# Attention and MLP on one core: attention steps as one skewed stream, groups of varied size, loads reordered, k of the first tiles on a second DMA queue

## The chip, the cores and the metric

One Trainium2 chip, one of its cores. The metric is the device time of one execution in microseconds (us). Executions of one kernel mostly agree within 1%; times below are medians of all runs of a kernel. A run that is more than 1.5% above the fastest of its kernel is called slow and is left out of the ratios. The span of a profiled execution is 1.7 to 2.1 us shorter than its time, so medians are compared with medians and spans with spans. Engines: PE (matmul), DVE (vector), ACT (scalar), POOL (GpSimd), SP (issues DMAs).

## The reference, cut to what matters

Block-wise linear attention with decay per head, then layer norm, a two-layer MLP with relu and a residual.

```python
# q, k, v: (4, 8, 768, 64) f32; lam: (8,)
# attention, in blocks, per batch and head:
#   out = ((q k^T) * decay_mask) v  +  (q * lam^(i+1)) S
#   S   = lam^block * S + (k * lam^(block-1-j))^T v
# x = out, heads side by side: (4, 768, 512)
xn = (x - mean) / sqrt(var + 1e-6) * g_ln
out = x + relu(xn @ w_ch1) @ w_ch2        # 512 -> 2048 -> 512, float32 out
```

Of the kernel before, what the change touches and what calls it, by code (L numbers as in the profile page):

```python
# [7 lines left out]
F32 = mybir.dt.float32  # L8
BF16 = mybir.dt.bfloat16
I32 = mybir.dt.int32  # L10
ALU = mybir.AluOpType
ACT = mybir.ActivationFunctionType
# [4 lines left out]
def kernel(  # L17
# [11 lines left out]
    nc = tc.nc  # L29
    B, H, S, D = q.shape  # L30
    C = 128
    nb = S // C
    NT = B * nb
    DM = H * D
    DF = moe_w_ch1.shape[1]
    NP = H // 2
    KA = DM // 128
    KB = DF // 128
    GT = 4
    NG = NT // GT  # L40
    NWC = 4
# [3 lines left out]
    ctx.enter_context(tc.manual_schedule())  # L45

    const = ctx.enter_context(tc.tile_pool(name="const", bufs=1))
    wst = ctx.enter_context(tc.tile_pool(name="wst", bufs=4))
    inp = ctx.enter_context(tc.tile_pool(name="inp", bufs=6))
    wk = ctx.enter_context(tc.tile_pool(name="wk", bufs=3))  # L50
    xp = ctx.enter_context(tc.tile_pool(name="xp", bufs=12))
    gp = ctx.enter_context(tc.tile_pool(name="gp", bufs=2))
    ps = ctx.enter_context(tc.tile_pool(name="ps", bufs=1, space=PSUM))

# [3 lines left out]
    def load_tile(t):  # L58
        b, c = divmod(t, nb)
        got = []  # L60
        for name, src in (("q", q), ("k", k), ("v", v)):
            f = inp.tile([128, H, D], F32, tag=name + "in", name=name + "in")
            nc.sync.dma_start(f, src[b, :, c * C:(c + 1) * C, :].rearrange("h p d -> p h d"))
            got.append(f)
        qkv_in[t] = got

    w1 = const.tile([128, KA, DF], BF16)
    w2 = const.tile([128, KB, DM], BF16)
    w_stage = {}
    W1C = DF // NWC  # L70
    W2K = KB // NWC

    def load_w1(c):
        f = wst.tile([128, KA, W1C], F32, tag="wst", name="w1f")
        nc.sync.dma_start(f, moe_w_ch1[:, c * W1C:(c + 1) * W1C].rearrange("(k p) f -> p k f", p=128))
        w_stage["w1", c] = f

    def load_w2(c):
        f = wst.tile([128, W2K, DM], F32, tag="wst", name="w2f")
        nc.sync.dma_start(f, moe_w_ch2[c * W2K * 128:(c + 1) * W2K * 128, :].rearrange("(k p) d -> p k d", p=128))  # L80
        w_stage["w2", c] = f

    def cast_w1(c):
        f = w_stage.pop(("w1", c))
        for kk in range(KA):
            dst = w1[:, kk, c * W1C:(c + 1) * W1C]
            if kk % 2 == 0:
                nc.vector.tensor_scalar_mul(dst, f[:, kk, :], g_col[:, kk:kk + 1])
            else:
                nc.scalar.mul(dst, f[:, kk, :], g_col[:, kk:kk + 1])  # L90

    def cast_w2(c):
        f = w_stage.pop(("w2", c))
        hk = W2K // 2
        nc.vector.tensor_copy(w2[:, c * W2K:c * W2K + hk, :], f[:, 0:hk, :])  # L95
        nc.gpsimd.tensor_copy(w2[:, c * W2K + hk:(c + 1) * W2K, :], f[:, hk:, :])

    lam_b = const.tile([128, H], F32)
    nc.sync.dma_start(lam_b, lam[None, :].to_broadcast([128, H]))
    load_tile(0)  # L100
    g_col = const.tile([128, KA], F32)
    nc.sync.dma_start(g_col, moe_g_ln.rearrange("(k p) -> p k", p=128))
    load_tile(1)
    load_w1(0)
    load_tile(2)
    load_tile(3)
    load_w1(1)
    load_w1(2)
    load_w1(3)


    ident = const.tile([128, 128], BF16)
    nc.gpsimd.memset(ident, 0.0)
    nc.gpsimd.affine_select(
        out=ident, in_=ident, compare_op=ALU.not_equal, fill=1.0,
# [5 lines left out]
        out=tril, in_=tril, compare_op=ALU.is_ge, fill=0.0,  # L121
# [35 lines left out]
    xT_of = {}  # L157

    def bf_inputs(t):
        qf, kf, vf = qkv_in.pop(t)  # L160
        qb = wk.tile([128, H, D], BF16, tag="qb", name="qb")
        nc.gpsimd.tensor_copy(qb, qf)  # L162
        kb = wk.tile([128, H, D], BF16, tag="kb", name="kb")
        nc.gpsimd.tensor_copy(kb, kf)  # L164
        vb = wk.tile([128, H, D], BF16, tag="vb", name="vb")
        nc.gpsimd.tensor_tensor(vb, vf, lam_v[:, :, None].to_broadcast([128, H, D]), op=ALU.mult)  # L166
        st[t] = dict(qb=qb, kb=kb, vb=vb)

    def p1(t):
        s = st[t]  # L170
        tp = ps.tile([128, 2, NP, 128], BF16, tag="aux", bufs=2, name="tp")
        for i, src in enumerate((s["kb"], s["qb"])):
            for p in range(NP):
                nc.tensor.transpose(tp[:, i, p, :], src[:, 2 * p:2 * p + 2, :], ident)  # L174
        kT = kTp[t % 2]
        nc.scalar.copy(kT[0:64, :, 0, :], tp[0:64, 0, :, :])  # L176
        qT = wk.tile([128, NP, 128], BF16, tag="qT", name="qT")
        nc.vector.tensor_copy(qT, tp[:, 1, :, :])  # L178
        nc.scalar.copy(kT[64:128, :, 1, :], tp[64:128, 0, :, :])  # L179
        s["kT"], s["qT"] = kT, qT  # L180

    def p2(t):
# [53 lines left out]

    def p4(t):
        s = st.pop(t)
        g, i = divmod(t, GT)
        if i == 0:  # L240
            xT_of[g] = gp.tile([128, KA, GT * 128], BF16, tag="xT", name="xT")
        xt = ps.tile([128, KA, 128], BF16, tag="aux", bufs=2, name="xt")
        for kk in range(KA):
            nc.tensor.transpose(xt[:, kk, :], s["xc"][:, kk * 128:(kk + 1) * 128], ident)  # L244
        nc.scalar.copy(xT_of[g][:, :, i * 128:(i + 1) * 128], xt)  # L245


    def mlp_units(g):
        hT = gp.tile([128, KB, GT * 128], BF16, tag="hT", name="hT")

        def m1(n):
            p1_ = ps.tile([128, GT * 128], F32, tag="mm", bufs=3, name="pm1")
            for kk in range(KA):
                nc.tensor.matmul(p1_, lhsT=w1[:, kk, n * 128:(n + 1) * 128], rhs=xT_of[g][:, kk, :],  # L254
                                 start=(kk == 0), stop=(kk == KA - 1))
            nc.scalar.activation(hT[:, n, :], p1_, ACT.Relu)  # L256

        acc = {}

        def m2(i, part):  # L260
            t = g * GT + i
            if part == 0:
                acc[i] = ps.tile([128, DM], F32, tag="mm", bufs=3, name="pm2")
            for kk in range(part * 4, part * 4 + 4):
                nc.tensor.matmul(acc[i], lhsT=hT[:, kk, i * 128:(i + 1) * 128], rhs=w2[:, kk, :],  # L265
                                 start=(kk == 0), stop=(kk == KB - 1))
            if part == KB // 4 - 1:
                x, rstd = x_keep.pop(t)
                o = wk.tile([128, DM], F32, tag="o", name="o")
                nc.vector.scalar_tensor_tensor(o, in0=acc.pop(i), scalar=rstd, in1=x, op0=ALU.mult, op1=ALU.add)  # L270
                b, c = divmod(t, nb)
                nc.sync.dma_start(out[b, c * C:(c + 1) * C, :], o)

        for n in range(KB):
            yield lambda n=n: m1(n)
        for i in range(GT):
            for part in range(KB // 4):
                yield lambda i=i, part=part: m2(i, part)


    def p01(t):
        if t + 1 < NT:
            bf_inputs(t + 1)
        p1(t)

    def att_steps(tiles):
        n = len(tiles)
        seq = []
        for j in range(n + 1):
            if j < n:  # L290
                seq.append((p01, tiles[j]))
            if j > 0:
                seq.append((p4, tiles[j - 1]))
            if j < n:
                seq.append((p2, tiles[j]))
                seq.append((p3, tiles[j]))
        return seq

    next_load = [4]

    def load_next():
        if next_load[0] < NT:
            load_tile(next_load[0])
            next_load[0] += 1


    load_next()
    bf_inputs(0)
    for f, t in att_steps(list(range(GT))):
        f(t)  # L310
    cast_w1(0)
    load_w2(0)
    load_next()
    load_w2(1)
    load_next()
    load_w2(2)
    load_next()
    load_w2(3)
    load_next()

    for g in range(NG):
        tiles = list(range((g + 1) * GT, min((g + 2) * GT, NT)))
        steps = att_steps(tiles)
        units = list(mlp_units(g))
        for u, unit in enumerate(units):
            if g == 0:
                if u % 4 == 0 and u // 4 + 1 < NWC:
                    cast_w1(u // 4 + 1)
                if u in (6, 9, 12, 15):
                    cast_w2(u // 3 - 2)  # L330
            if u % 8 == 0:
                load_next()
            unit()
            if u % 2 == 1 and u // 2 < len(steps):
                f, t = steps[u // 2]
                f(t)
        for f, t in steps[len(units) // 2:]:
            f(t)


# [28 lines left out]
```

## The kernel before: the parts that the change touches

The kernel works on 24 tiles of 128 rows (6 per sequence). `bf_inputs` casts a tile's q, k, v to bf16 on POOL (qb, kb, vb); `p1` transposes k and q on PE and copies them out (kT, qT); `p2` makes the masked scores mA and the state S; `p3` makes the output x and its norm (xc); `p4` transposes the normed x (xT). In the MLP pm is a matmul's PSUM tile and hT the hidden layer. Groups of four tiles then go through the MLP, with the attention of the next group interleaved between units of four matmuls of 512 columns.

```python
def bf_inputs(t):
    qf, kf, vf = qkv_in.pop(t)
    nc.gpsimd.tensor_copy(qb, qf)                                   # POOL
    nc.gpsimd.tensor_copy(kb, kf)                                   # POOL
    nc.gpsimd.tensor_tensor(vb, vf, lam_v[...], op=ALU.mult)        # POOL
# ...
def p2(t):
    # scores on PE, two mA on DVE, state product pk on PE ...
    if c == 0:                                                      # first tile of a sequence
        nc.vector.tensor_tensor(Sn, pk, lamC, op=ALU.mult)
    else:
        nc.vector.tensor_tensor(tmp, pk, state["S"], op=ALU.add)    # Stmp, DVE
        nc.gpsimd.tensor_tensor(Sn, tmp, lamC, op=ALU.mult)         # Sn, POOL
# (the last tile of a sequence has no Sn)
# ...
def p01(t):
    if t + 1 < NT:
        bf_inputs(t + 1)      # the casts of the NEXT tile come first
    p1(t)

# per tile, in program order: p01(t), p4(t-1), p2(t), p3(t)
for g in range(NG):           # six groups of four
    for u, unit in enumerate(units):
        # ... casts of weights in the first group, next load ...
        unit()
        if u % 2 == 1 and u // 2 < len(steps):
            f, t = steps[u // 2]
            f(t)
```

## Time and profile before

| | before |
|---|---|
| median of 4 runs | 259.62 us (258.76 to 262.1) |
| span of the profiled execution | 258.8 us |
| busy: PE, DVE, ACT, POOL | 86%, 53%, 42%, 31% |
| first MLP matmul | 34.4 us |
| first MLP group | 45.8 us |
| four groups of four tiles | 36.7 to 36.9 us each |
| last group, and the last store | 27.8 and 3.8 us |

The prediction shows how these are read out of the chain of waits. Columns of the timeline: start, duration (us), engine, line, operation, output and input, shape, count, and in brackets the idle time before it and what ended it.

### The profile page before, as it was taken

How to read it: one execution, taken by the hardware profiler on the slowest of the kernel's cores; microseconds unless marked ns; L12 is line 12 of the kernel's file. 1: busy time of each engine (PE TensorE's matmuls, PEld its weight loads, DVE VectorE, ACT ScalarE, POOL GpSimd, SP SyncE). 2: the span in 40 equal slices, each digit the busy share in tenths (PEclk: the TensorE clock that was granted, in tenths of full speed). 3: DMA queues.
4: the chain of work that ended last, by engine and by line, in shares of the span. 5: the costliest groups of instructions: out<-in, count | busy, mean ns of one | idle time of the engine just before them, and what ended most of it. 6: DMA issues, size and time to landing. Idle time of an engine off the chain costs nothing.

```text
span 258.8 us, 4115 instructions
## 1 busy us (share of the span) xinstructions
PE 223.7 (86%) x1600; PEld 122.3 (47%) x1600; DVE 137.8 (53%) x256; ACT 108.9 (42%) x207; POOL 81.0 (31%) x101
## 2 busy tenths in 40 slices
PE   0666479695997999989999979999979999989994
PEld 0444235352553555545555535555535555444441
DVE  3467766762753746773475664548547467600121
ACT  5332266743114664306662326761146742066200
POOL 3546052754413523740051352810145131000000
PEclk9999759998899999999999999999999999999999
DMA  6999929999999920279901549601210002110022
GB/s 128 273 227 360 270 64 292 254 276 287 218 241 252 222 56 0 84 162 203 203 2 43 127 120 228 136 0 43 81 42 3 0 3 81 41 43 0 0 81 81
DMA packets 83250, 33.81 MB, mean 131 GB/s; under 512 B 76064, under 2 KB 76064, under 8 KB 83232
## 3 DMA queue, kind: packets, MB, share of 16 engines
q1 hardware_dynamic: 83232, 33.57, 55.8%
q8 instruction: 12, 0.20, 0.3%
q14 instruction: 6, 0.05, 0.1%
HBM read 27.27 MB, written 6.29 MB: 130 GB/s over the span
## 4 chain that ended last, share of the span: by engine, by line
PE 66%; DVE 16%; ACT 9%; DMA 4%; issue 2%; POOL 1%; SPq 1%; POOLq 0%
PE pm L265 28%; PE pm L254 23%; PE sc L190 4%; DVE stats L225 4%; DVE x L222 4%; PE tp L174 3%; DMA w2f<-in_moe_w_ch_dram 3%; ACT hT L256 2%; DVE mA L192 2%; ACT kTp L179 2%; PE po L215 2%; PE po L219 2%; PE xt L244 2%; DVE xc L229 2%; DMA kin<-in_k_dram 2%
## 5 line engine op out<-in xcount | busy, mean ns | idle before, releaser
L254 PE MATMUL pm<-xT,w 128*128 128x512 bf16 x384 | 92.3, 384 | 6.9 <-ACT xT L245 4.0
L265 PE MATMUL pm<-w,hT 128*128 128x512 bf16 x384 | 90.9, 382 | 3.0 <-DVE w L95 2.7
L256 ACT ACTIVATE hT<-pm 128x512 bf16<-128x512 f32 x96 | 54.4, 597 | 19.7 <-PE pm L254 19.5
L254 PEld LDWEIGHTS <-w 128*128 128x128 bf16 x384 | 36.3, 99 | 45.5 <-issue 9.2
L265 PEld LDWEIGHTS <-hT 128*128 128x128 bf16 x384 | 36.0, 98 | 39.6 <-issue 3.7
L207 POOL TENSOR_TENSOR Sn<-Stmp,lamC 128x512 bf16<-128x512 f32 x16 | 20.6, 1289 | 98.9 <-DVE Stmp L206 50.4
L270 DVE SCALAR_TENSOR_TENSOR o<-pm,rstd,x 128x512 f32<-128x512 f32 x24 | 17.8, 741 | 48.2 <-PE pm L265 48.2
L231 ACT ACTIVATE std<-mv,eps_t 128x1 f32<-128x1 f32 x24 | 7.1, 294 | 85.2 <-DVE mv L227 85.2
L192 DVE TENSOR_TENSOR mA<-sc,tril 128x512 bf16<-128x512 f32 x48 | 30.8, 683 | 22.3 <-PE sc L190 22.3
L166 POOL TENSOR_TENSOR vb<-vin,lam_v 128x512 bf16<-128x512 f32 x24 | 25.9, 1079 | 6.9 <-issue 4.4
L178 DVE COPY qT<-tp 128x512 bf16<-128x512 bf16 x24 | 10.1, 422 | 24.1 <-ACT kTp L176 24.1
L222 DVE TENSOR_TENSOR x<-po,lam_q 128x512 f32<-128x512 f32 x24 | 16.6, 690 | 11.6 <-PE po L219 9.8
L162 POOL CAST qb<-qin 128x512 bf16<-128x512 f32 x24 | 15.2, 632 | 19.6 <-DMA qin<-in_q_dram 19.6
L190 PE MATMUL sc<-qT,kTp 128*128 128x128 bf16 x192 | 17.8, 234 | 3.2 <-DVE qT L178 1.7
L179 ACT COPY kTp<-tp 64x512 bf16<-64x512 bf16 x24 | 13.9, 580 | 15.5 <-DVE qT L178 15.5
L229 DVE TENSOR_SCALAR xc<-x,mv 128x512 bf16<-128x512 f32 x24 | 18.4, 767 | 0.9
L244 PE MATMUL xt<-ident,xc 128*128 128x128 bf16 x96 | 10.0, 231 | 10.2 <-DVE xc L229 10.2
L190 PEld LDWEIGHTS <-kTp 128*128 128x128 bf16 x192 | 13.7, 104 | 10.8 <-ACT kTp L179 5.3
L225 DVE BATCH_NORM_STATS2 stats<-x 128x6 f32<-128x512 f32 x24 | 16.7, 694 | 0.8
L245 ACT COPY xT<-xt 128x512 bf16<-128x512 bf16 x24 | 14.1, 587 | 6.1 <-PE xt L244 5.9
L174 PE MATMUL tp<-ident,kb 128*128 128x128 bf16 x96 | 10.5, 238 | 6.9 <-POOL kb L164 6.9
L164 POOL CAST kb<-kin 128x512 bf16<-128x512 f32 x24 | 15.2, 632 | 3.5 <-DMA kin<-in_k_dram 2.9
(42 smaller groups left out, 146.9 us busy)
## 6 DMA issues: line engine op xcount, KB each, us to landing
qin<-in_q_dram SPq DMA_DIRECT2D x24, 256.0 KB, 5.0
kin<-in_k_dram SPq DMA_DIRECT2D x24, 256.0 KB, 5.3
vin<-in_v_dram SPq DMA_DIRECT2D x24, 256.0 KB, 5.1
out_dram<-o SPq DMA_DIRECT2D x24, 256.0 KB, 2.0
w1f<-in_moe_w_ch_dram SPq DMA_DIRECT2D x4, 1024.0 KB, 7.5
w2f<-in_moe_w_ch_dram SPq DMA_DIRECT2D x4, 1024.0 KB, 6.8
lam_b<-in_lam_dram SPq DMA_DIRECT2D x1, 4.0 KB, 2.8
g_col<-in_moe_g_ln_dram SPq DMA_DIRECT2D x1, 2.0 KB, 4.1
```

What stands on the lines that cost most here:

```text
L166: nc.gpsimd.tensor_tensor(vb, vf, lam_v[:, :, None].to_broadcast([128, H, D]), op=ALU.mult)
L174: nc.tensor.transpose(tp[:, i, p, :], src[:, 2 * p:2 * p + 2, :], ident)
L179: nc.scalar.copy(kT[64:128, :, 1, :], tp[64:128, 0, :, :])
L190: nc.tensor.matmul(sc[:, i, :], lhsT=s["kT"][:, h // 2, h % 2, :], rhs=s["qT"][:, h // 2, :], start=(i == 0), stop=(i == H // 2 - 1), skip ...
L192: nc.vector.tensor_tensor(mA[:, half * (H // 2):(half + 1) * (H // 2), :], sc, tril[:, None, :].to_broadcast([128, H // 2, 128]), op=ALU.mult)
L207: nc.gpsimd.tensor_tensor(Sn, tmp, lamC, op=ALU.mult)
L222: nc.vector.tensor_tensor(x.rearrange("p (h d) -> p h d", h=H), po, lam_q[:, :, None].to_broadcast([128, H, D]), op=ALU.mult)
L225: nc.vector.bn_stats(stats, x)
L229: nc.vector.tensor_scalar(xc, x, mv[:, 0:1], None, op0=ALU.subtract)
L254: nc.tensor.matmul(p1_, lhsT=w1[:, kk, n * 128:(n + 1) * 128], rhs=xT_of[g][:, kk, :], start=(kk == 0), stop=(kk == KA - 1))
L256: nc.scalar.activation(hT[:, n, :], p1_, ACT.Relu)
L265: nc.tensor.matmul(acc[i], lhsT=hT[:, kk, i * 128:(i + 1) * 128], rhs=w2[:, kk, :], start=(kk == 0), stop=(kk == KB - 1))
```

## The change

Intent: PE should not wait at the end of a group. The attention steps become one list for all tiles, skewed by one tile (p3 of tile t-1 after p1 of tile t, so that PE need not wait for mA), and spread evenly over the units of a group. The second group has only tiles 4 and 5 and the last only 22 and 23. w2 gets two more staging buffers and is loaded early; weight casts are spread over three engines; k of tiles 0 to 3 is issued from ACT; q and k are transposed into separate PSUM tiles (tq and tk). The buffers of hT go from two to one and those of xp from 12 to 11. The core of the diff:

```diff
-    wst = ctx.enter_context(tc.tile_pool(name="wst", bufs=4))
+    wst = ctx.enter_context(tc.tile_pool(name="wst", bufs=6))
@@ load_tile
-            nc.sync.dma_start(f, src[...])
+            eng = nc.scalar if name == "k" and t < 4 else nc.sync
+            eng.dma_start(f, src[...])
@@ cast_w1: kk 0 and 2 on DVE, 1 on ACT
+            else:
+                nc.gpsimd.tensor_scalar_mul(dst, f[:, kk, :], g_col[:, kk:kk + 1])   # kk 3
@@ loads: ... tile 3, w1 0, w1 1, tile 4, w1 2, w1 3
+    for c in range(NWC):
+        load_w2(c)
+    load_tile(5)
@@ p1: tk (k, with ACT's two copies), then tq (q, with DVE's copy), for the one tile tp
@@ schedule
+    groups = [[0, 1, 2, 3], [4, 5]]          # then fours, then [22, 23]
+    def p0(t):
+        if t + 5 < NT and t > 0:
+            load_tile(t + 5)
+        bf_inputs(t)
+    for j in range(NT + 1):
+        # (the round behind the first group has its own order; cut)
+        steps.append((p1, j))
+        steps.append((p3, j - 1))
+        steps.append((p2, j))
+        steps.append((p0, j + 1))
+        steps.append((p4, j - 1))
# ... steps spread over the units of a group, all but the last two; weight casts of the
# first group three units ahead of use; second layer of the first group part by part;
# last tile's output in two halves
```

More of the change, by code (lines that the diff above doesn't have):

```diff
@@ L47 @@
     const = ctx.enter_context(tc.tile_pool(name="const", bufs=1))
-    wst = ctx.enter_context(tc.tile_pool(name="wst", bufs=4))
+    wst = ctx.enter_context(tc.tile_pool(name="wst", bufs=6))
     inp = ctx.enter_context(tc.tile_pool(name="inp", bufs=6))
     wk = ctx.enter_context(tc.tile_pool(name="wk", bufs=3))
-    xp = ctx.enter_context(tc.tile_pool(name="xp", bufs=12))
+    xp = ctx.enter_context(tc.tile_pool(name="xp", bufs=11))
     gp = ctx.enter_context(tc.tile_pool(name="gp", bufs=2))
@@ L62, in load_tile @@
             f = inp.tile([128, H, D], F32, tag=name + "in", name=name + "in")
-            nc.sync.dma_start(f, src[b, :, c * C:(c + 1) * C, :].rearrange("h p d -> p h d"))
+            eng = nc.scalar if name == "k" and t < 4 else nc.sync
+            eng.dma_start(f, src[b, :, c * C:(c + 1) * C, :].rearrange("h p d -> p h d"))
             got.append(f)
@@ L88, in cast_w1 @@
                 nc.vector.tensor_scalar_mul(dst, f[:, kk, :], g_col[:, kk:kk + 1])
+            elif kk == 1:
+                nc.scalar.mul(dst, f[:, kk, :], g_col[:, kk:kk + 1])
             else:
-                nc.scalar.mul(dst, f[:, kk, :], g_col[:, kk:kk + 1])
+                nc.gpsimd.tensor_scalar_mul(dst, f[:, kk, :], g_col[:, kk:kk + 1])
     def cast_w2(c):
         f = w_stage.pop(("w2", c))
-        hk = W2K // 2
-        nc.vector.tensor_copy(w2[:, c * W2K:c * W2K + hk, :], f[:, 0:hk, :])
-        nc.gpsimd.tensor_copy(w2[:, c * W2K + hk:(c + 1) * W2K, :], f[:, hk:, :])
+        for i in range(W2K):
+            dst = w2[:, c * W2K + i, :]
+            if i % 2 == 0:
+                nc.vector.tensor_copy(dst, f[:, i, :])
+            elif i == 1:
+                nc.scalar.copy(dst, f[:, i, :])
+            else:
+                nc.gpsimd.tensor_copy(dst, f[:, i, :])
     lam_b = const.tile([128, H], F32)
@@ L103 @@
     load_tile(1)
-    load_w1(0)
     load_tile(2)
     load_tile(3)
+    load_w1(0)
     load_w1(1)
+    load_tile(4)
     load_w1(2)
     load_w1(3)
+    for c in range(NWC):
+        load_w2(c)
+    load_tile(5)
     ident = const.tile([128, 128], BF16)
@@ L170, in p1 @@
         s = st[t]
-        tp = ps.tile([128, 2, NP, 128], BF16, tag="aux", bufs=2, name="tp")
-        for i, src in enumerate((s["kb"], s["qb"])):
-            for p in range(NP):
-                nc.tensor.transpose(tp[:, i, p, :], src[:, 2 * p:2 * p + 2, :], ident)
+        tk = ps.tile([128, NP, 128], BF16, tag="aux", bufs=2, name="tk")
+        for p in range(NP):
+            nc.tensor.transpose(tk[:, p, :], s["kb"][:, 2 * p:2 * p + 2, :], ident)
         kT = kTp[t % 2]
-        nc.scalar.copy(kT[0:64, :, 0, :], tp[0:64, 0, :, :])
+        nc.scalar.copy(kT[0:64, :, 0, :], tk[0:64, :, :])
+        nc.scalar.copy(kT[64:128, :, 1, :], tk[64:128, :, :])
+        tq = ps.tile([128, NP, 128], BF16, tag="aux", bufs=2, name="tq")
+        for p in range(NP):
+            nc.tensor.transpose(tq[:, p, :], s["qb"][:, 2 * p:2 * p + 2, :], ident)
         qT = wk.tile([128, NP, 128], BF16, tag="qT", name="qT")
-        nc.vector.tensor_copy(qT, tp[:, 1, :, :])
-        nc.scalar.copy(kT[64:128, :, 1, :], tp[64:128, 0, :, :])
+        nc.vector.tensor_copy(qT, tq)
         s["kT"], s["qT"] = kT, qT
@@ L238, in p4 @@
         s = st.pop(t)
-        g, i = divmod(t, GT)
+        g = group_of[t]
+        i = t - groups[g][0]
         if i == 0:
@@ L248, in mlp_units @@
     def mlp_units(g):
-        hT = gp.tile([128, KB, GT * 128], BF16, tag="hT", name="hT")
+        hT = gp.tile([128, KB, GT * 128], BF16, tag="hT", bufs=1, name="hT")
+        n_t = len(groups[g])
+        N = n_t * 128
         def m1(n):
-            p1_ = ps.tile([128, GT * 128], F32, tag="mm", bufs=3, name="pm1")
+            pm = ps.tile([128, GT * 128], F32, tag="mm", bufs=3, name="pm1")
             for kk in range(KA):
-                nc.tensor.matmul(p1_, lhsT=w1[:, kk, n * 128:(n + 1) * 128], rhs=xT_of[g][:, kk, :],
+                nc.tensor.matmul(pm[:, 0:N], lhsT=w1[:, kk, n * 128:(n + 1) * 128], rhs=xT_of[g][:, kk, 0:N],
                                  start=(kk == 0), stop=(kk == KA - 1))
-            nc.scalar.activation(hT[:, n, :], p1_, ACT.Relu)
+            nc.scalar.activation(hT[:, n, 0:N], pm[:, 0:N], ACT.Relu)
         acc = {}
         def m2(i, part):
-            t = g * GT + i
+            t = groups[g][i]
             if part == 0:
@@ L269, in m2 @@
                 o = wk.tile([128, DM], F32, tag="o", name="o")
-                nc.vector.scalar_tensor_tensor(o, in0=acc.pop(i), scalar=rstd, in1=x, op0=ALU.mult, op1=ALU.add)
                 b, c = divmod(t, nb)
-                nc.sync.dma_start(out[b, c * C:(c + 1) * C, :], o)
-        for n in range(KB):
-            yield lambda n=n: m1(n)
-        for i in range(GT):
-            for part in range(KB // 4):
-                yield lambda i=i, part=part: m2(i, part)
-    def p01(t):
-        if t + 1 < NT:
-            bf_inputs(t + 1)
-        p1(t)
@@ L286, in att_steps @@
-    def att_steps(tiles):
-        n = len(tiles)
-        seq = []
-        for j in range(n + 1):
-            if j < n:
-                seq.append((p01, tiles[j]))
-            if j > 0:
-                seq.append((p4, tiles[j - 1]))
-            if j < n:
-                seq.append((p2, tiles[j]))
-                seq.append((p3, tiles[j]))
-        return seq
-    next_load = [4]
-    def load_next():
-        if next_load[0] < NT:
-            load_tile(next_load[0])
-            next_load[0] += 1
@@ L307 @@
-    load_next()
-    bf_inputs(0)
-    for f, t in att_steps(list(range(GT))):
-        f(t)
-    cast_w1(0)
-    load_w2(0)
-    load_next()
-    load_w2(1)
-    load_next()
-    load_w2(2)
-    load_next()
-    load_w2(3)
-    load_next()
-    for g in range(NG):
-        tiles = list(range((g + 1) * GT, min((g + 2) * GT, NT)))
-        steps = att_steps(tiles)
+                a = acc.pop(i)
+                n_p = 2 if t == NT - 1 else 1
+                w = DM // n_p
+                for z in range(n_p):
+                    sl = slice(z * w, (z + 1) * w)
+                    nc.vector.scalar_tensor_tensor(o[:, sl], in0=a[:, sl], scalar=rstd, in1=x[:, sl],
+                                                   op0=ALU.mult, op1=ALU.add)
+                    nc.sync.dma_start(out[b, c * C:(c + 1) * C, sl], o[:, sl])
@@ new lines, in mlp_units @@
+        for n in range(KB):
+            yield "m1", n, lambda n=n: m1(n)
+        lead = min(3, n_t) if g == 0 else 1
+        order = [(i, part) for part in range(KB // 4) for i in range(lead)]
+        order += [(i, part) for i in range(lead, n_t) for part in range(KB // 4)]
+        for i, part in order:
+            yield "m2", part, lambda i=i, part=part: m2(i, part)
+    groups = [[0, 1, 2, 3], [4, 5]]
+    while groups[-1][-1] < NT - 1:
+        f = groups[-1][-1] + 1
+        groups.append(list(range(f, min(f + GT, NT))))
@@ new lines @@
+    group_of = {t: g for g, ts in enumerate(groups) for t in ts}
+    def p0(t):
+        if t + 5 < NT and t > 0:
+            load_tile(t + 5)
+        bf_inputs(t)
+    steps = [(p0, 0)]
+    for j in range(NT + 1):
+        lone = j - 1 == groups[0][-1]
+        if j < NT and not lone:
+            steps.append((p1, j))
+        if j > 0:
+            steps.append((p3, j - 1))
+        if j < NT and not lone:
+            steps.append((p2, j))
+            if j + 1 < NT and j != groups[0][-1]:
+                steps.append((p0, j + 1))
+        if j > 0:
+            steps.append((p4, j - 1))
+        if lone:
+            steps += [(p0, j), (p1, j), (p2, j), (p0, j + 1)]
@@ L324, with upto, run_steps @@
+    def upto(g):
+        return steps.index((p4, groups[g][-1])) + 1 if g < len(groups) else len(steps)
+    pos = 0
+    def run_steps(end):
+        nonlocal pos
+        while pos < end:
+            f, t = steps[pos]
+            f(t)
+            pos += 1
+    run_steps(upto(0))
+    cast_w1(0)
+    w1_cast, w2_cast = 1, 0
+    for g in range(len(groups)):
         units = list(mlp_units(g))
-        for u, unit in enumerate(units):
+        first, end = pos, upto(g + 1)
+        span = len(units) - 2
+        for u, (kind, n, unit) in enumerate(units):
@@ L326 @@
             if g == 0:
-                if u % 4 == 0 and u // 4 + 1 < NWC:
-                    cast_w1(u // 4 + 1)
-                if u in (6, 9, 12, 15):
-                    cast_w2(u // 3 - 2)
-            if u % 8 == 0:
-                load_next()
-            unit()
-            if u % 2 == 1 and u // 2 < len(steps):
-                f, t = steps[u // 2]
-                f(t)
-        for f, t in steps[len(units) // 2:]:
-            f(t)
+                if kind == "m1" and n % 4 == 2 and w1_cast < NWC:
+                    cast_w1(w1_cast)
+                    w1_cast += 1
@@ L342 @@
+                if (kind == "m1" and n == KB - 1) or (kind == "m2" and w2_cast < NWC and n >= w2_cast - 1):
+                    cast_w2(w2_cast)
+                    w2_cast += 1
+            unit()
+            run_steps(min(end, first + ((end - first) * (u + 1)) // span))
 _INS = ['q', 'k', 'v', 'lam', 'moe_g_ln', 'moe_w_ch1', 'moe_w_ch2']
```

## The prediction

> **What bounds the kernel now.** I read the page first: busy shares, the slices, then the chain.
>
> ```profile
> PE 223.7 (86%) x1600; PEld 122.3 (47%) x1600; DVE 137.8 (53%) x256; ACT 108.9 (42%) x207; POOL 81.0 (31%) x101
> PE   0666479695997999989999979999979999989994
> DVE  3467766762753746773475664548547467600121
> POOL 3546052754413523740051352810145131000000
> ```
>
> PE is the bound from about 65 us on; before that no engine is full, so the start is a chain of waits. The chain in order of time cuts the 258.8 us: first MLP matmul at 34.4; first MLP group to 80.2 (45.8 us); four groups of 36.7 us each (80.18, 116.84, 153.78, 190.48, 227.14); a last group of 27.8 us without attention; 3.9 us of last eviction and store. One MLP group of four tiles is thus 27.8 us of pure PE (6.95 per tile). From the timeline, attention of a warm tile takes PE 0.45 (eight transposes) + 0.45 (scores) + 0.22 (state) + 0.45 (outputs) + 0.22 (x transposes) = 1.79 us, 1.57 where the state or its use is missing: 1.72 on average. A full group needs 27.8 + 4 x 1.72 = 34.7, so 2.0 us per group are lost, at the boundary:
>
> ```profile
> 150.22 0.70 DVE x L222
> 150.95 0.70 DVE stats L225
> 151.89 0.76 DVE xc L229
> 153.14 0.59 ACT xT L245
> 153.78 1.89 PE pm L254 x8
> ```
>
> The chain leaves PE here: the new group's first matmul waits for the last tile's norm, transposes and copy. The first group loses 45.8 - 34.7 = 11 us to casts, the late last piece of w2 (landing at 61.5) and a cold clock. The start runs at 6.3 us a tile, bound by waits between DVE, ACT and PE. In the timeline, tile 1 and the POOL queue at a later group end:
>
> ```profile
> 16.27 1.29 DVE L192 TENSOR_TENSOR mA<-sc,tril 128x512 bf16<-128x512 f32 x2 [1.21 <-PE sc L190]
> 17.47 0.68 DVE L206 TENSOR_TENSOR Stmp<-pk,Sn 128x512 f32<-128x512 f32 x1
> ...
> 186.69 1.27 POOL L207 TENSOR_TENSOR Sn<-Stmp,lamC 128x512 bf16<-128x512 f32 x1 [16.03 <-PE po L215]
> ...
> 187.91 0.61 POOL L162 CAST qb<-qin 128x512 bf16<-128x512 f32 x1
> ...
> 188.46 0.61 POOL L164 CAST kb<-kin 128x512 bf16<-128x512 f32 x1
> ```
>
> POOL idles 16 us ahead of Sn, and qb and kb, whose inputs are long there, start only behind it. What stands behind Sn in POOL's program waits for it. Before, this costs little: a tile's casts are issued a whole tile ahead of use.
>
> **What the Trainium skill says.** "TensorE: Matmul & The Clock Gate", Architectural detail: the queues of ACT and DVE are strict FIFO, GPSIMD's is strict FIFO per core. The 16.03 us above agree. The same page, Part 1: after about 3.4 us without work PE falls to half clock and needs about 3.4 us of activity to recover. The trace agrees: four transposes take 0.61 us in the start and 0.39 later, and the first eight MLP matmuls 3.79 us against 1.89. "DMA: Bandwidth & Descriptors", Issuing engines are not separate DMA queues: a second issuing engine saves only issue time, the 16 engines are shared. Before has one issuing queue, so no line tests it; but issues stretch to about 1.14 us per 256 KB early on, which is 230 GB/s, so the engines look full. I give the second queue no gain.
>
> **The change part by part.**
>
> *Order of the casts.* Each round now is p1(t), p3(t-1), p2(t), p0(t+1), p4(t-1). p2 puts Sn(t) on POOL; p0(t+1), the casts of the next tile, comes behind it; the next step but one is p1(t+1), which needs them. Before, the casts of t+1 stood ahead of p1(t). So for tiles 1 to 4 of each sequence (their Sn is on POOL; tile 0's is on DVE, tile 5 has none) a loop closes: x chain of t-1 to the end of the reciprocal 2.2 to 2.4 us (12.04 to 14.26, 150.22 to 152.64), two mA 1.21 (16.27 to 17.47), Stmp to Sn 0.76, Sn 1.21 to the next start, qb 0.55, kb to PE 0.67: 6.7 us from x to the transposes. Added are transposes (1.1 cold, 0.6 warm) and qT 0.46 before the next x: 8.3 us a tile.
>
> *The start.* Tile 0 as before: scores at about 10.2, DVE free at 12.1. q of tile 1 lands at about 10.7, as k of four tiles shares the engines; transposes at 11.95, qT 13.1, x 13.5, Sn1 at 17.8, qT2 at 21.3, qT3 at 29.6, Stmp3 at 33.6, x3 34.3, xc3 36.5, xT3 37.8. First MLP matmul at 37.9, against 34.4. Splitting the transposes into two PSUM tiles removes ACT-DVE-ACT alternation (ACT and DVE reads of one tile ran one after the other, 0.5 us twice a tile), but that was on the old loop, not on the new one.
>
> *First group.* PE work 27.8 + 3.4 (tiles 4, 5) + 1.1 (first steps of tile 6) = 32.3. Cold start 2.0, as before (3.79 against 1.73 per eight). w2 goes early into two more buffers, and its order is part by part, so the wait at 59 to 62 goes. Tile 5 is issued behind the last w2 piece, though; 13.1 MB at the 265 to 278 GB/s of the early slices land at about 50, near its use: 1.5 us. w2's first cast stands behind mA5 on DVE: 1.3 us. Sum 37.1, end at 75.0.
>
> *Group of tiles 4 and 5.* PE has 13.9 us of MLP and 4 x 1.72 of attention: 20.8. But four rounds run in it, with about one unit per step and half-width first-layer units of 0.43 us. From x start to the next transposes PE has -0.2 + 0.43 + 0.67 + 3 x 0.43 + 0.22 = 2.4 us of work, the loop needs 6.7: stall 4.3. The next rounds give 3.9, 3.5 and 0.8, with more second-layer units in them. 12.5 us, plus 2 of cold clock after such gaps: 35.3, end at 110.3.
>
> *Three groups of four.* Steps are spread 20 over 30 units of 0.864 us. From x to the next transposes PE has -0.2 + 6 x 0.864 + 0.67 + 0.22 = 5.9, the loop 6.75: 0.85 of stall, 1.6 in the third round, where an o eviction (0.75) stands before mA; none in the fourth, which has the group end's extra units. Counting blocked tiles only (13; 15, 16; 19, 20, 21): 1.6 + 1.7 + 3.3 = 6.6. The boundary wait goes: p4 ends two units ahead. 3 x 27.8 + 12 x 1.72 + 6.6 = 110.6, end at 220.9.
>
> *End.* Tiles 18 to 21: 27.8 + 2.3 = 30.1, at 251.0. Tiles 22, 23: 13.9, at 264.9. Tail 3.6, the halved last output saving perhaps 0.3: 268.5. That a short last group shortens a tail is no gain: the old one had PE full.
>
> **The rivals.** First: the skew wins. If the casts were not held by Sn (their inputs are there, and POOL is busy only 31%), the start would be bound by DVE: qT 0.42, x to reciprocal 2.3, mA 1.2, Stmp 0.7 make 4.7 us a tile, first MLP at about 27; the group stalls vanish (-8 against before) and the first group loses some 5 instead of 11: about 237. Against it stands the line with 16.03. Second: the loop exists but is milder by 1 us a tile, with the weaker stalls hidden: about 5 fewer in the three groups, 3 fewer in the short group, 2 in the start: 258, within 2%. For it: PE is in order, so a stall in one round gives slack in the next. Third: DMA becomes the bound of the first 50 us, as k on the other queue delays v and q, and tile 5 holds up POOL, and behind it the w1 cast: some 3 to 5 us more, about 272. For it: DMA is nine tenths busy there.
>
> **Range and chances.** The sum gives 268.5. I take 266, since errors in the loop lie more towards rival two and a tuned-looking schedule may hide what I count singly. Range 252 to 276: rivals two and three with something over. Faster by over 2% (below 254.5) needs the first rival or the loop short by more than 1 us: 0.14. Within 2%: 0.29. Slower: 0.57.
>
> **What would show it.** Right: the first MLP matmul at 36 to 40 us; PE's transposes waiting for POOL kb with waits of 3 to 5 us in the short group (75 to 110) and about 1 us later; POOL's qb starting right behind Sn; boundaries without a wait for xT; the last two groups dense. Wrong: a first MLP matmul before 32 us, qb starting ahead of Sn of the tile before, or no transposes waiting for kb past 80 us; then the loop isn't there and the time is near 240.

## More of the kernel before

One more view is needed later: POOL's rows of the timeline of the kernel before, in the start.

```profile
15.31 0.61 POOL L162 CAST qb<-qin 128x512 bf16<-128x512 f32 x1 [3.19 <-DMA qin<-in_q_dram]
16.52 0.61 POOL L164 CAST kb<-kin 128x512 bf16<-128x512 f32 x1 [0.59 <-DMA kin<-in_k_dram]
17.74 1.04 POOL L166 TENSOR_TENSOR vb<-vin,lam_v 128x512 bf16<-128x512 f32 x1 [0.61 <-DMA vin<-in_v_dram]
18.74 1.26 POOL L207 TENSOR_TENSOR Sn<-Stmp,lamC 128x512 bf16<-128x512 f32 x1
```

The casts here are those of tile 2, and the Sn behind them is that of tile 1. The casts run as soon as their loads land and nobody waits for them.

## The result, and the profile after

The changed kernel is correct and slower: 271.63 us, median of 4 runs (270.84 to 273.23), against 259.62 us. The ratio is 1.0454 (95% interval 1.0369 to 1.054). Ratios here are the mean time of one kernel's fast runs over that of the other's fast runs of the same rounds, so not quite the ratio of the medians. The time lies inside the predicted range.

Stages of the two profiled executions, cut at the first MLP matmul of each group, beside the sum of the prediction:

| stage (us) | before | predicted | after |
|---|---|---|---|
| up to the first MLP matmul | 34.4 | 37.9 | 40.7 |
| first group | 45.8 | 37.1 | 39.0 |
| tiles 4, 5 | | 35.3 | 32.9 |
| groups of four with full attention beside them | 147.0 (four) | 110.6 (three) | 109.3 (three) |
| tiles 18 to 21 | | 30.1 | 30.0 |
| last group | 27.8 (four tiles) | 13.9 (two) | 14.2 (two) |
| last eviction and store | 3.8 | 3.6 | 3.9 |
| sum | 258.8 | 268.5 | 270.0 |

PE's wait for kb in the kernel before, then the two largest waits of PE in the changed kernel, and then POOL's largest (columns: who waited for whom, us in total, times, longest):

```profile
PE tp L174 <- POOL kb L164: 6.9, 1, 6.9
```

```profile
PE tk L185 <- POOL kb L176: 30.0, 14, 8.1
PE xt L259 <- DVE xc L243: 5.1, 6, 2.3
```

```profile
POOL Sn L221 <- DVE Stmp L220: 130.4, 16, 20.8
```

In the kernel before PE waited for POOL's kb once, 6.9 us, for the first load. Now it waits 14 times. And all 16 Sn that are on POOL now hold that engine until DVE has made Stmp, with the casts behind them. The timeline of the group of tiles 4 and 5 shows one turn of the loop:

```profile
85.28 0.68 DVE L220 TENSOR_TENSOR Stmp<-pk,Sn 128x512 f32<-128x512 f32 x1
86.04 1.26 POOL L221 TENSOR_TENSOR Sn<-Stmp,lamC 128x512 bf16<-128x512 f32 x1 [20.84 <-DVE Stmp L220]
87.25 0.61 POOL L174 CAST qb<-qin 128x512 bf16<-128x512 f32 x1
87.80 0.61 POOL L176 CAST kb<-kin 128x512 bf16<-128x512 f32 x1
...
88.47 0.40 PE L185 MATMUL tk<-ident,kb 128*128 128x128 bf16 x4 [3.47 <-POOL kb L176]
...
90.02 0.69 DVE L236 TENSOR_TENSOR x<-po,lam_q 128x512 f32<-128x512 f32 x1 [0.47 <-PE po L233]
...
92.17 1.27 DVE L206 TENSOR_TENSOR mA<-sc,tril 128x512 bf16<-128x512 f32 x2
...
93.35 0.68 DVE L220 TENSOR_TENSOR Stmp<-pk,Sn 128x512 f32<-128x512 f32 x1
```

From Stmp to Stmp it is 8.07 us. POOL idles 20.84 us with the loads of the next tile long landed; then Sn, qb, kb follow within 2.4 us and PE starts 0.06 us after kb. The next such waits of PE are 3.03, 2.43 and 0.29 us, with more matmul work in the later rounds. In the three groups of four behind it (112.6 to 223) PE waits for kb seven times; the 0.29 is one of the seven:

```profile
PE tk L185 <- POOL kb L176: 4.6, 7, 1.2
```

The wait for xT at the group ends, 0.7 us and its transposes ahead of it, is gone.

The start is where the result is worst against the sum. Its lines: the second queue, the first table load of ACT, and of tile 1 the cast of q and the transposes of q:

```profile
0.78 5.57 ACTq L64 DMA_DIRECT2D kin<-in_k_dram  x4
...
6.38 1.28 ACT L153 ACT_TABLE_LOAD   x1 [6.38 <-DMA kin<-in_k_dram]
...
11.86 0.61 POOL L174 CAST qb<-qin 128x512 bf16<-128x512 f32 x1 [1.24 <-DMA qin<-in_q_dram]
...
14.96 0.58 PE L191 MATMUL tq<-ident,qb 128*128 128x128 bf16 x4 [1.27 <-ACT kTp L188]
```

The cast of the same q in the kernel before:

```profile
8.80 0.61 POOL L162 CAST qb<-qin 128x512 bf16<-128x512 f32 x1 [0.17 <-DMA qin<-in_q_dram]
```

ACT stands behind its own four issues until 6.38 us. Before, its first table load was at 0.80. So lam_c, kT and the first scores come late. But q of tile 1 also lands 3.1 us later than before (the cast waits for it until 11.86, not 8.80), and the k transposes of tile 1 start at 13.08, right behind its casts and right behind tile 0's work on PE. Which of the two cost the time no run separates.

### The profile page after: what moved, and what is told of

It reads as the page before. It is cut to its first block, busy times and chain, and to the rows that moved or that the text cites. A ratio compares the mean times of both kernels' runs of the same rounds, so it can differ in the third digit from the quotient of the medians.

```text
span 270.0 us, 4247 instructions
## 1 busy us (share of the span) xinstructions
PE 221.7 (82%) x1638; PEld 128.6 (48%) x1664; DVE 132.7 (49%) x261; ACT 113.2 (42%) x223; POOL 82.8 (31%) x105
## 5 line engine op out<-in xcount | busy, mean ns | idle before, releaser
L271 PE MATMUL pm<-xT,w 128*128 128x512 bf16 (+1 forms) x435 | 93.8, 356 | 2.8 <-POOL w L93 1.1
L282 PE MATMUL pm<-w,hT 128*128 128x512 bf16 x371 | 88.6, 379 | 2.3 <-DVE w L100 1.6
L273 ACT ACTIVATE hT<-pm 128x512 bf16<-128x512 f32 (+1 forms) x112 | 58.3, 534 | 26.1 <-PE pm L271 24.3
L271 PEld LDWEIGHTS <-w 128*128 128x128 bf16 x448 | 42.8, 100 | 36.4 <-issue 3.0
L282 PEld LDWEIGHTS <-hT 128*128 128x128 bf16 x384 | 35.9, 98 | 38.3 <-DVE w L100 2.1
L193 DVE COPY qT<-tq 128x512 bf16<-128x512 bf16 x24 | 10.2, 424 | 58.8 <-PE tq L191 58.8
L185 PE MATMUL tk<-ident,kb 128*128 128x128 bf16 x96 | 10.3, 235 | 30.0 <-POOL kb L176 30.0
L293 DVE SCALAR_TENSOR_TENSOR o<-pm,rstd,x 128x512 f32<-128x512 f32 (+1 forms) x25 | 17.9, 724 | 32.8 <-PE pm L282 32.8
L187 ACT COPY kTp<-tk 64x512 bf16<-64x512 bf16 x24 | 13.8, 575 | 30.2 <-PE tk L185 30.1
L185 PEld LDWEIGHTS <-kb 128*128 128x128 bf16 x96 | 6.6, 103 | 37.7 <-POOL kb L176 35.8
L204 PE MATMUL sc<-qT,kTp 128*128 128x128 bf16 x192 | 17.0, 237 | 2.5 <-DVE qT L193 2.4
L204 PEld LDWEIGHTS <-kTp 128*128 128x128 bf16 x192 | 14.2, 107 | 7.5 <-ACT kTp L188 1.7
L259 PE MATMUL xt<-ident,xc 128*128 128x128 bf16 x96 | 10.2, 234 | 5.2 <-DVE xc L243 5.1
```

What stands on the lines that cost most here:

```text
L185: nc.tensor.transpose(tk[:, p, :], s["kb"][:, 2 * p:2 * p + 2, :], ident)
L204: nc.tensor.matmul(sc[:, i, :], lhsT=s["kT"][:, h // 2, h % 2, :], rhs=s["qT"][:, h // 2, :], start=(i == 0), stop=(i == H // 2 - 1), skip ...
L271: nc.tensor.matmul(pm[:, 0:N], lhsT=w1[:, kk, n * 128:(n + 1) * 128], rhs=xT_of[g][:, kk, 0:N], start=(kk == 0), stop=(kk == KA - 1))
L273: nc.scalar.activation(hT[:, n, 0:N], pm[:, 0:N], ACT.Relu)
L282: nc.tensor.matmul(acc[i], lhsT=hT[:, kk, i * 128:(i + 1) * 128], rhs=w2[:, kk, :], start=(kk == 0), stop=(kk == KB - 1))
L293: nc.vector.scalar_tensor_tensor(o[:, sl], in0=a[:, sl], scalar=rstd, in1=x[:, sl], op0=ALU.mult, op1=ALU.add)
```

## The experiments

The theory after the result: on POOL, Sn(t) stands ahead of the casts of tile t+1, so a loop closes (Stmp, Sn, qb, kb, transposes, qT, x chain, mA, Stmp) that sets the pace wherever PE has less than that much work to do. Rivals: the loss comes from the other parts (the second queue, the half-width group, weight casts on POOL), or from the casts being late in the program whatever stands before them. All runs below are correct; each ratio is against the kernel before on the same chip.

### e1: the casts ahead of Sn

```diff
-            steps.append((p2, j))
-            if j + 1 < NT and j != groups[0][-1]:
-                steps.append((p0, j + 1))
+            early = j + 1 < NT and j != groups[0][-1]
+            steps.append((p02 if early else p2, j))     # p02(t): p0(t + 1), then p2(t)
+            if early:
+                steps.append((skip, j + 1))             # does nothing: keeps PE's order
```

(and the same in the lone round behind the first group)

> The changed kernel with the casts of tile t+1 put on POOL ahead of p2(t) and so ahead of Sn(t); the order of work on PE is exactly that of the changed kernel. Theory (the loop Sn, qb, kb, transposes, x chain, mA, Stmp, Sn sets the pace): the 30 us in which PE waits for POOL kb fall to a few us; the start runs at DVE's pace, some 4.9 us a tile instead of 8.4, first MLP matmul at about 33 instead of 40.7; the group of tiles 4 and 5 takes about 23 us instead of 32.9; about 249 us in all. Rival (the loss comes from the k loads on ACT's queue, the POOL weight casts and the half-width matmuls, and the waits for kb would be replaced by equal waits for DVE): 266 us or more.

Measured: 254.87 us (253.97 to 255.24, 4 runs), ratio 0.9774 (0.9724 to 0.9823). PE's longest wait in the profile:

```profile
PE tk L185 <- POOL kb L176: 9.0, 2, 8.1
```

Two waits are left, the first load (8.1) and one of 0.8. The span is 253.1 us: this one swap takes 16.9 us off the changed kernel (270.0) and makes it faster than the kernel before; whether by 2% is unclear, as the interval reaches over 0.98. First MLP matmul at 36.1 (40.7), group of tiles 4 and 5 in 24.2 us (32.9), and from there to the end 151.6 us (157.4). The first group is longer, 41.1 us (39.0), as PE waits there 2.6 us for a w1 piece on POOL. The rival is out. But I expected 249: the start came to 36.1 and not 33 (e6 and e12 say why: the queue, and a PSUM buffer), and the first group grew.

### e2: k back on the one queue

```diff
-            eng = nc.scalar if name == "k" and t < 4 else nc.sync
-            eng.dma_start(f, src[...])
+            nc.sync.dma_start(f, src[...])
```

> The changed kernel with all k loads back on the one queue. Theory: the second queue was no gain but a loss, as ACT stood behind its four issues until 6.38 us and its tables and copies came 2 to 2.5 us late for tile 0; the first scores return from 11.6 to about 9.5, and the total falls by 2 to 3 us to about 269. Rival (the second queue speeds the loads): the total rises by 1 us or more.

Measured: 270.19 us (269.55 to 270.28, 4 runs), ratio 1.0361 (1.0311 to 1.0411). In its timeline ACT loads its table at 0.78 us and the scores start at 8.47:

```profile
0.78 1.28 ACT L152 ACT_TABLE_LOAD   x1 [0.78 <-PEq L376]
...
8.47 1.26 PE L203 MATMUL sc<-qT,kTp 128*128 128x128 bf16 x8 [0.52 <-DVE qT L192]
```

The first MLP matmul moves from 40.7 to 38.3, so 2.4 us of the start were the queue's doing. Both delays go at once: ACT starts at 0.78 and q of tile 1 is cast at 8.80 again, so the run doesn't say which of them it was. The spans differ by 2.2 us (267.8 and 270.0), with the first group at 39.0 us in both; the medians differ by 1.4, as the profiled run of e2 is the fastest of its four. The direction is as the theory has it, the size rather small.

### e3: groups of four in the changed kernel

```diff
-    groups = [[0, 1, 2, 3], [4, 5]]
+    groups = [[0, 1, 2, 3]]
```

> The changed kernel with all groups of four tiles (casts behind Sn and k on ACT's queue as in the change). Theory: the loop costs most where a round has the least matmul work to lie beside, so the 9 us of waits for kb in the group of tiles 4 and 5, and its half-width matmuls, go, each blocked round costing 0.5 to 1.2 us instead of 2.4 to 3.5; about 261 us. Rival (the loop costs about the same per tile whatever the group): within 3 us of the changed kernel.

Measured: 269.87 us (269.07 to 271.84, 6 runs), ratio 1.0346 (1.0286 to 1.0405). A miss by 9 us: the number is the rival's. The profile says that the rival's reason isn't: in the later groups PE waits for kb only 4.7 us in all (1.5 + 2.1 + 1.1), as expected. It is the first group that takes 53.2 us:

```profile
49.29 1.43 POOL L221 TENSOR_TENSOR Sn<-Stmp,lamC 128x512 bf16<-128x512 f32 x1 [5.10 <-DVE Stmp L220]
52.30 0.61 POOL L174 CAST qb<-qin 128x512 bf16<-128x512 f32 x1 [1.58 <-DMA qin<-in_q_dram]
54.04 0.61 POOL L176 CAST kb<-kin 128x512 bf16<-128x512 f32 x1 [1.14 <-DMA kin<-in_k_dram]
54.72 0.61 PE L185 MATMUL tk<-ident,kb 128*128 128x128 bf16 x4 [4.40 <-POOL kb L176]
```

Tile 5 is loaded behind the last piece of w2, and its q and k land at 52.3 and 54.0; with four attention tiles beside the first group it is wanted some 4 us earlier. PE waits 4.4 us, and its matmuls then run cold, that is at a slower pace (0.61 us for four transposes that take 0.39 later). PE also waits there 2.2 us for the kb of a later tile and 2.0 us for a w2 piece, so tile 5 is the longest wait but not the whole loss. The short group seems to have a purpose that I had not credited: it keeps attention out of the group whose transfers are late. No run shows that alone.

### e4: Sn on DVE, casts as late as in the change

```diff
-                nc.gpsimd.tensor_tensor(Sn, tmp, lamC, op=ALU.mult)
+                nc.vector.tensor_tensor(Sn, tmp, lamC, op=ALU.mult)
```

> The changed kernel with every Sn on DVE, so that nothing on POOL waits for DVE; the casts stay in their late place in the program. Theory (POOL held by Sn): the waits for kb nearly vanish though the casts are as late in the program as before, and DVE pays 0.7 us a tile for it: first MLP matmul at about 36, about 252 us in all. Rival (what hurts is that the casts come late in the program, Sn or no Sn): the waits for kb stay above 20 us and the total above 265 us.

Measured: 253.08 us (252.78 to 253.37, 4 runs), ratio 0.971 (0.9664 to 0.9756). PE's waits for kb:

```profile
PE tk L185 <- POOL kb L176: 9.2, 2, 8.1
```

The casts are where the change put them, and apart from the first load (8.1) PE waits 1.1 us for them in all. So it isn't their place in the program but the one operation ahead of them that waits for another engine. DVE has room for 0.7 us a tile more.

### e5: the order of the change alone, in the kernel before

```diff
-    def p01(t):
-        if t + 1 < NT:
-            bf_inputs(t + 1)
-        p1(t)
+    def p20(t):              # in p2's place; p1 in p01's
+        p2(t)
+        if t + 1 < NT:
+            bf_inputs(t + 1)
```

> The kernel before with one thing of the change alone: the casts of tile t+1 come behind p2(t), and so behind Sn(t), on POOL. Theory: PE's transposes begin to wait for POOL kb here too, about 3 us a tile in the start for tiles 2 to 4 with first MLP matmul at about 38 instead of 34.4, and about half a microsecond in the later rounds; 265 to 270 us in all, as slow as the whole change. Rival (the order hurts only together with the skewed stream and the groups): within 2 us of the kernel before.

Measured: 267.63 us (265.38 to 268.52, 4 runs), ratio 1.0249 (1.017 to 1.0328); slower, though whether by 2% is unclear. In its timeline, tile 2:

```profile
18.27 1.26 POOL L207 TENSOR_TENSOR Sn<-Stmp,lamC 128x512 bf16<-128x512 f32 x1 [6.08 <-DVE Stmp L206]
19.48 0.61 POOL L162 CAST qb<-qin 128x512 bf16<-128x512 f32 x1
20.03 0.61 POOL L164 CAST kb<-kin 128x512 bf16<-128x512 f32 x1
20.70 0.61 PE L174 MATMUL tp<-ident,kb 128*128 128x128 bf16 x4 [2.23 <-POOL kb L164]
```

Transposes follow each other at 7.77 us (20.70, 28.47), where they did at 6.3, and the first MLP matmul is at 37.8, as expected. Moving the casts is enough to make a kernel without any other part of the change 7.3 us longer in the profile. The loop here is of the same kind but not link for link: p3 comes behind p2, so the x chain lies beside it and not in it.

### e6, e7, e8: from e1 towards a better version

e6 is e1 with the edit of e2. e7 also takes w1 off POOL; e8 also loads tile 5 ahead of w2:

```diff
-            elif kk == 1:
-                nc.scalar.mul(...)
-            else:
-                nc.gpsimd.tensor_scalar_mul(...)
+            else:                       # e7: kk 1 and 3 on ACT, as before the change
+                nc.scalar.mul(...)
@@ e8
+    load_tile(5)
     for c in range(NWC):
         load_w2(c)
-    load_tile(5)
```

> Casts ahead of Sn, and k on the one queue again. Theory (independent costs, start only): the 1.4 us that the k queue cost in the changed kernel come off here too, about 253.3 us against 254.9. Rival (start bound by something else once the loop is gone): no difference.

Measured: 252.9 us (251.47 to 253.41, 4 runs), ratio 0.9694 (0.964 to 0.9749). First MLP matmul 34.3 (36.1 in e1). The queue's cost comes off here too, 2.0 us.

> As the one before, and the w1 pieces that the change put on POOL are back on ACT. Theory: the 2.6 us in which PE waits for POOL's w1 piece, which stands behind the casts of the late tile 5, go, and ACT has room; about 251 us. Rival: PE then waits the same time for kb of tile 5 or for ACT's pieces; no difference.

Measured: 250.12 us (249.13 to 251.64, 4 runs), ratio 0.9602 (0.9544 to 0.966). The group that went, in e1 (line, engine, operation, count, busy us, mean ns):

```profile
L93 POOL TENSOR_SCALAR w<-w1f,g_col 128x512 bf16<-128x512 f32 x4 | 6.7, 1670 | 0.0
```

A w1 piece takes 1.67 us on POOL; the cast of the same shape there takes 0.66, and the w1 piece on ACT 0.72. The first group shrinks from 41.4 us (e6) to 37.4.

> As the one before, and tile 5 is loaded ahead of w2 instead of behind it. Theory: tile 5 then lands near 40 us and no engine waits for it; w2's pieces still land before 62. First group about 2 us shorter, about 249 us. Rival: w2's last pieces come later in turn and PE waits for w2; no gain or a loss.

Measured: 249.97 us (249.78 to 251.36, 4 runs), ratio 0.9602 (0.955 to 0.9654). No gain. PE's wait for tile 5's kb (1.5 us in e7) is gone; in its place PE waits 1.8 us for a w2 piece on POOL and 1.1 us for one on DVE. The piece on POOL stands behind the casts of tile 6, for whose load POOL waits 5.0 us, until 51.4. So no gain, as the rival had it, but it isn't w2's own transfer that PE waits for.

### e9: groups of four, once the loop and the late tile 5 are gone

Edit: e8 with the edit of e3.

> The last kernel (casts first, k on the one queue, w1 on ACT, tile 5 early) with all groups of four. Theory: with the loop and the late tile 5 gone, the short group costs some 4 us over its matmul work (24.8 us for 20.8) and groups of four some 1 us at most; against that the first group has two tiles more beside its casts. 247 to 250 us, within 1% of the version with the short group; and unlike the earlier run with groups of four, no wait of several us for tile 5. Rival (the short group is what makes the first group bearable): 254 us or more.

Measured: 250.2 us, median of 4 runs; the fast ones are 249.29, 250.08 and 250.32, ratio 0.9564 (0.9479 to 0.9648). Groups of four and the short group are equal here, as expected, so the loss of e3 was not in the groups themselves. That it was tile 5 alone isn't separated from the loop by this run, since both edits are in it.

### e10, e11, e12: what holds the start

These three build on e8. In e1 the transposes of q wait 1.3 us twice for ACT's copies of the same tile's k. I took this to be the PSUM buffer: q's transposes being given the one of k. e10 issues them ahead of ACT's copies; e11 also moves the first w2 cast; e12 gives the two PSUM buffers separate names.

```diff
@@ e10: in p1, ACT's two copies of tk moved behind the transposes of q
@@ e11
-                if (kind == "m1" and n == KB - 1) or ...
+                if (kind == "m1" and n == KB - 4) or ...
@@ e12: tk and pk share one buffer, tq and xt the other
-   tag="aux", bufs=2    (tk, pk, tq, xt)
+   tag="auxk", bufs=1   (tk, pk)        tag="auxq", bufs=1   (tq, xt)
```

> The version before this with the short group, and the transposes of q issued ahead of ACT's two copies of kT in program order, so that tq is not given the PSUM buffer that tk has just used. Theory: the two waits of 1.3 us of tq for ACT's kTp in the start go, first MLP matmul at about 31.8 instead of 34.2, about 247.5 us. Rival: tq then waits for another reader of the same two buffers and the start stays at 34.

Measured: 249.26 us (248.75 to 250.48, 5 runs), ratio 0.9532 (0.945 to 0.9615). The wait is still there:

```profile
PE tq L185 <- ACT kTp L188: 2.6, 2, 1.3
```

First MLP matmul at 34.5, no gain in the start. The order in the program doesn't decide which buffer tq gets: in the trace, the first q transpose of tile 2 still waits for ACT's second copy of k of the same tile.

> As e10, and the first w2 cast is issued three units earlier, at unit 12 of the first layer. Theory: the 2.9 us in which PE's second layer waits for POOL's and DVE's w2 pieces in the first group shrink to below 1; about 245.5 us. Rival: DVE and POOL are busy with tile 5 there, and the cast delays mA and the casts of tile 6 in turn; no gain.

Measured: 248.45 us (248.03 to 249.46, 4 runs), ratio 0.9514 (0.9442 to 0.9586), the lowest median of all, though its interval and that of e10 overlap. The first group takes 35.1 us (38.2 in e10) and PE no longer waits for w2 in it; but the group of tiles 4 and 5 takes 26.1 us (24.2), where PE now waits 1.7 us for qT on DVE. Of 3.1 us won, 1.9 are given back one group later.

> As e11, with the two small PSUM buffers tied to their use: tk and pk share one, tq and xt the other, so tq can never be given the buffer of tk of the same tile. Theory (the buffer choice makes tq wait for kT's copies): the two waits of 1.3 us of tq for ACT's kTp go, first MLP matmul at about 32 instead of 34.6, about 246 us. Rival: tk then waits for Stmp or tq for xT instead, for as long; first MLP at 34 or later, no gain.

Measured: 248.89 us (248.31 to 250.9, 7 runs), ratio 0.9545 (0.9504 to 0.9585). The wait of tq for kTp is gone, so it was the buffer, and the first MLP matmul is at 32.3. The end isn't earlier:

```profile
PE tk L182 <- DVE Stmp L217: 4.7, 5, 1.2
PE pm L279 <- POOL w L101: 2.4, 1, 2.4
```

POOL now stands 7.1 us ahead of the casts of tile 6, until 52.7 us, for a load behind w2, with a w2 piece of its own behind those casts; PE waits 2.4 us for that piece. In e11 the same casts start at 51.2. PE came earlier, the transfers didn't. (The profiled execution of e12 is the slowest of its seven, 250.9 us; the medians of e11 and e12 are 0.4 us apart.) Versions e7 to e12 lie within 1% of each other; against the kernel before, the best (e11) is 4.9% faster by its ratio, and it is some 23 us below the changed kernel.

## Why the prediction was right

Its mechanism, the loop, is shown; its total is nearer than its parts. Against the profiled span of 270.0 the sum of 268.5 is 1.5 us short, but the start and the first group were 4.7 us too low and the short group and the three groups 3.7 us too high, so a good part of the agreement is cancelling errors. The 266 took another 2.5 us off for errors in the loop; the loop was over-counted indeed, but the missing terms weighed more (4.7 against 3.7). Of the signs that it named, the first MLP matmul at 36 to 40 us was missed by 0.7, and the waits of 3 to 5 us in the short group were 2.4 to 3.5; the others came. By its own steps:

- **The loop.** Right, and close in size. Predicted 8.3 us a tile in the start; qT of tiles 2 and 3 are at 23.61 and 32.05, 8.44 apart. e1 and e4 open the loop in two ways and both remove the waits; e5 closes one like it in the other kernel and brings them there.
- **The start, 37.9 against 40.7.** Terms were missing. I gave the second queue no gain and counted only a later q of tile 1, at 10.7. It came at 11.86, and ACT's four issues took 5.57 us of its own time, which I had not counted and which put the first scores at 11.58 where I had 10.2. The transposes of tile 1 began at 13.08 for 11.95; e2 takes off 2.4 us. And tile 1's tq stood 1.3 us behind ACT's copy (e10, e12), which I hadn't seen.
- **The first group, 37.1 against 39.0.** The waits for the late tile (0.9 for 1.5) and for w2 (1.6 for 1.3) are there. The w1 pieces on POOL, 1.68 us each, were not in the sum; PE waits 1.1 for one of them, and e7 shows what they cost once the loop is gone.
- **Tiles 4 and 5, 35.3 against 32.9.** The waits are 3.47, 3.03, 2.43 and 0.29, for my 4.3, 3.9, 3.5 and 0.8: I over-counted each by 0.5 to 1.1. And only a part of the 2 us of cold clock came: four transposes still take 0.40 after the wait of 3.47; after that of 3.03 eight half-width matmuls run at the slow pace.
- **Three groups, 110.6 against 109.3.** Besides the 0.29, which I had put into the short group, there are six waits, as many as predicted, with 4.3 us in all for 6.6. The first two rounds of a group wait 0.49 where I had 0.85, the third 1.15 where I had 1.6.
- **The end** as counted; the halved last output gave nothing visible (3.9 us, and 3.8 before).
- **The rivals.** The first, the skew winning at about 237, named what is lost if the loop isn't there, and its number was far off: without the loop it is 253 to 255 (e4, e1). It took the start to be bound by DVE's 4.7 us a tile; in e1 qT of tiles 1 to 3 comes every 5.5 to 6.5 us, with waits for ACT's copies and PSUM buffers in between. The third, the transfers, was partly there: k on the other queue goes with a q of tile 1 that lands 3.1 us later, and tile 5 is late, with the w1 cast behind it. The total of about 272 that it named is nearer to the measured 271.63 than the 266.

So the change was two things of opposite sign. Everything but the order of the casts is worth 5.7 us in the profiles (258.8 to 253.1 in e1), and the place of three casts on POOL costs 16.9. Without the queue and the w1 pieces on POOL, which cost time themselves, the rest is worth 11.5 us (247.3 in e7); the skew, the early w2 and the group ends weren't measured apart. In the kernel before the same order costs 7.3 us only (e5).

## What to carry to other kernels

When work is reordered for one engine, write down the new order of every engine, and look in each in-order queue for an operation that waits for another engine with work behind it that needs nothing: that work becomes a link of the loop, however idle its engine is. The dearest place for such a loop is the stage with the least other work per turn, so measure it there and not by the average. And a gain in the start has to be followed to the next shared limit, here the transfers of the first 53 us, before it is counted.

## What the Trainium skill lacked or had wrong

- "DMA: Bandwidth & Descriptors", Issuing engines are not separate DMA queues: the page says that the time to issue is usually small beside the transfer and that a second issuing engine saves only this time. What it lacks is that issues can be long and hold the issuing engine's own work: four issues of 256 KB took ACT 5.57 us, 1.4 us each, where issues of this size from SP took 0.37 to 0.44 us around 88 us, and ACT's first operation came at 6.38 instead of 0.80. With the queue taken back (e2) the start is 2.4 us shorter, in which an earlier q of tile 1 may have its part.
- "GPSIMD Engine Reference", Engine selection: one-input operations are called roughly line-rate there. A cast of 128x512 took 0.66 us on POOL, but the one-input multiply by a scalar per partition 1.67 to 1.68 us, against 0.72 on ACT and 0.74 on DVE.
- "TensorE: Matmul & The Clock Gate", Architectural detail: the strict FIFO that it states for POOL agrees with the trace (casts behind one operation that waited 20.84 us). No page draws the consequence that the casts behind a waiting operation close a loop between engines; it was 16.9 us of 270 here.
- The same page, Seeing it yourself (HAM trace caveats): it warns that recorded clock events can be unreliable, and this looks like an instance: the clock of the changed kernel's first 40.7 us is recorded as 1.00, and four transposes in it take 0.61 us, against 0.39 later.
